# A new written-out order of the events, 126 more events on another engine, and 31 fewer products of zeros, in a kernel of delta-rule attention and a feed-forward layer

## The chip, the cores and the metric

The kernel runs on one core of one Trainium2 chip. A core has five engines that work from queues of their own: TensorE (PE in the profile, its weight loads are PEld), VectorE (DVE), ScalarE (ACT), GpSimd (POOL) and SyncE (SP, which issues every DMA here). An engine takes the instructions of its queue in order, and waits for others by semaphores. The metric is the time of one execution on the chip in microseconds; lower is better.

## The reference

Two parts, one behind the other (the inputs are random; batch 4, 8 heads, 768 positions, 48 numbers a head):

```python
k_n = k / (np.linalg.norm(k, axis=-1, keepdims=True) + 1e-06)
for t in range(S):                                   # delta rule, state 48 x 48 a head
    y[:, :, t] = np.einsum('bhd,bhde->bhe', q[:, :, t], state)
    v_old = np.einsum('bhde,bhd->bhe', state, kt)
    state = state + bt[:, :, :, None] * np.einsum('bhd,bhe->bhde', kt, vt - v_old)
...
h = x @ w_in                                         # x: 3072 x 384, w_in: 384 x 2048
sp = np.maximum(h, 0.0) + np.log1p(np.exp(-np.abs(h)))
return ((h * erf(sp)) @ w_out).astype(np.float32)    # w_out: 2048 x 384
```

## The kernel before

The sequence is cut into 12 chunks of 64 positions. For a chunk c the kernel squares and sums the keys (`norm_sq` on ScalarE, `norm_sum` and six `norm_ops` on VectorE), forms products of keys and queries on TensorE (`gram_mm`), scales and masks them on VectorE (`gram_a`, `gram_p`), and turns the triangular system of the delta rule into an inverse. For that the blocks go through DRAM (`to_dram`, `to_blocks`), are solved for two chunks at a time, 31 rows one after the other with two instructions a row (`solve_row(sg, s)`, lines 355 and 357: the first pair of chunks on VectorE, the other five pairs on GpSimd), and come back by TensorE transposes (`back_t`, copies `back_x`) or by DRAM (`put_blocks`, `from_blocks2`). Steps named `merge_` then put four 32-wide blocks of a chunk together. A chain over the chunks follows, four batches a chunk (j = 4c + b): `put_v` (values times norms, GpSimd), `chain_u`, `chain_s`, `chain_y` on TensorE, with `chain_u2`, `chain_s2` on VectorE, `chain_y2` (a copy out of PSUM) on ScalarE.

The feed-forward layer works on 12 groups of 256 positions. The output of group g is scaled by a power of two that is found on the way (`x_max`, `x_all`, `x_scale`) and split into two fp16 parts, `x_hi` (ScalarE) and `x_lo` (VectorE). `ffn1(n)` is nine fp16 matmuls of 256 columns (line 697), one `ffn1` for each 128 of the 2048 columns of w_in. For two of them at a time ScalarE takes softplus out of PSUM (`e_sp`) and erf of it (`e_erf`), which live in different function tables: going from one to the other costs a table load (line 165). VectorE multiplies (`e_mul`), the product is cast to fp16 (`e_split`, ScalarE or VectorE) and the rest of the cast is formed (`e_rest`, VectorE or GpSimd). `ffn2(n)` is six fp16 matmuls of 384 columns (lines 749 to 751). The weights come in as 64-bit numbers, 12 pieces of each matrix; a piece is put together from its halves by `w_mask`, `w_sign` (ScalarE), `w_bits` (VectorE), its largest value found by `w_mx` (ScalarE, or a reduction on VectorE), and after `w_max`, `w_all`, `w_scale` it is split into fp16 parts (`w_hi`, and `w_lo1` on TensorE with `w_lo2`, or `w_lo` on VectorE).

Products of a tile of zeros (`fill` into a buffer of its own, line 180; `fill2` into a bank of PSUM that ffn2 uses, line 186) stand in TensorE's queue where it would wait: their results are never read.

What sets the order: every step is registered as an event by `on(t, fn, ...)`, and gets the next number. Then `ORDER` lists the numbers, and the events are issued in that order, each engine taking what is its own. `ENG` names, by the event's number, those events that go to another engine than their function's own.

```python
ORDER = (1321,1,1276,1266,2,3,4,5, ...)      # 2481 numbers
ENG = {350: "G", 464: "V", 734: "A", ...}    # 17 entries
    def pick(d):
        return ENG.get(cur[0], d)
...
    for i in range(WU):
        on(us(6 + 0.17 * i), fill)
    for i in range(WV):
        on(us(6 + 0.17 * (WU + i)), fill2)
...
    ev = [ev[i] for i in ORDER] if ORDER else sorted(ev, key=lambda e: e[:2])
    with tc.manual_schedule(engines={E.PE, E.Activation, E.DVE, E.Pool, E.SP}):
        for _, i, fn in ev:
            cur[0] = i
            fn()
```

Of the kernel before, what the change touches and what calls it, by code (L numbers as in the profile page):

```python
# [34 lines left out]
ENG = {350: "G", 464: "V", 734: "A", 742: "A", 759: "V", 766: "A", 796: "A", 913: "V", 1027: "V", 1134: "V", 1295: "V", 1437: "V", 1441: "G", 1445: "G", 1639: "A", 1981: "V", 2151: "V"}  # L35
LEAD = 3
MD = 4.4
CS = 1.2
WARM = 15
C2 = 12.0  # L40
C3 = 16.0
SS2 = 12.8
S1 = -2.5
SPL = 32
XT = (0, 1)
UM = 32
DZ = 64
WG = -6
WU = 177
WV = 63  # L50
MT = 58
M1 = 0
WL = (0.9, 0.95, 1.0, 1.05, 1.1, 1.15, 24, 24.1, 31.0, 32.5, 34.0, 35.5)
WK = (6.0, 6.7, 7.4, 8.1, 8.8, 9.5, 28, 29, 36.0, 37.5, 39.0, 40.5)
WF = (6.6, 7.3, 8.0, 8.7, 9.4, 10.1, 28.6, 29.6, 36.6, 38.1, 39.6, 41.1)
WI = (17.0, 18.0, 19.0, 20.0, 21.0, 22.0, 31, 32, 50.5, 52.1, 53.7, 55.3)
WOT = (36, 38, 40, 42, 76, 78, 62, 86, 88, 90, 72, 74)
WD = 0.4
LPE = ("in",)
RI = "HLHLHLHLHLHH"  # L60
RO = "LHLHLHLHLHHH"
# [25 lines left out]
def delta_ffn_kernel(ctx, tc, kT, qT, ktok, vtok, btok, w_in, w_out, cst, out):  # L87
# [20 lines left out]
    def on(t, fn, *a, **kw):  # L108
        ev.append((t, len(ev), lambda: fn(*a, **kw)))
# [3 lines left out]
    def pick(d):  # L113

        return ENG.get(cur[0], d)

# [17 lines left out]
    def us(x):  # L134
        return (x - T0) / SW
# [671 lines left out]
    on(-98, warm, WARM)  # L807
# [4 lines that stand above are left out]
    on(us(0), clear_q)  # L812
# [179 lines left out]

    ev = [ev[i] for i in ORDER] if ORDER else sorted(ev, key=lambda e: e[:2])
    E = mybir.EngineType
# [47 lines left out]
```

## Time and profile before

| what | value |
|---|---|
| median of 3 runs | 613.57 us |
| lowest, highest | 609.68, 617.38 us |
| the profiled execution | 615.59 us |
| its span from first to last instruction | 613.8 us |
| busy share PE, ACT, DVE, POOL | 97%, 85%, 66%, 50% |
| TensorE's granted clock, mean over the span | 0.983 of full speed |
| table loads of ScalarE | 169 at line 165, 216.8 us |

The profiled execution has 1.8 us outside its span and is 2.0 us above the median. The rows further down come from this one execution. A busy TensorE is not one at its peak: a matmul's recorded duration (274 ns for 256 columns) is longer than the distance from one start to the next, so prices of TensorE's work are read from runs of matmuls in the chain that ended last.

### The profile page before, as it was taken

The page shows a single profiled execution, that of the slowest core. Times are in us where ns is not written, and L with a number is a line of the kernel's source. Part 1 is how long each engine was busy: PE and PEld are TensorE (multiplying, and loading weights), DVE is VectorE, ACT ScalarE, POOL GpSimd, SP SyncE. Part 2 cuts the span into 40 slices and gives each one's busy share as a digit, 9 for nine tenths or more (in the row PEclk, how much of TensorE's full clock was granted, in tenths as well). Part 3 has the DMA queues.
Part 4 walks back from the last instruction along what each step waited for, and adds up shares of the span by engine and source line. Part 5 has one row for each costly group of instructions (what it writes and reads, how often), then busy time and mean ns, then how long its engine had stood idle before and what let it go on. Part 6 is the DMA issues. An engine that isn't in the chain of part 4 may idle for free.

```text
span 613.8 us, 25249 instructions
## 1 busy us (share of the span) xinstructions
PE 595.4 (97%) x11019; PEld 426.9 (70%) x11019; DVE 403.8 (66%) x926; ACT 522.9 (85%) x751; POOL 307.8 (50%) x484
## 2 busy tenths in 40 slices
PE   9899989999999899999999999999999999999996
PEld 3654456667777677777777777777777777777773
DVE  0769986668787788887776977666565655436221
ACT  8859897999996789878968999897989797989873
POOL 3000313798589733998527884489953122213221
PEclk9799898999999899999999999999999999999999
DMA  9999625850755367624485226713045200100111
GB/s 313 281 235 350 152 52 124 226 141 28 185 105 142 93 163 153 156 63 117 92 212 140 67 66 148 148 50 91 1 115 121 53 17 21 27 2 14 27 27 26
DMA packets 86382, 69.72 MB, mean 114 GB/s; under 512 B 64064, under 2 KB 73408, under 8 KB 86272
## 3 DMA queue, kind: packets, MB, share of 16 engines
q1 hardware_dynamic: 86272, 68.12, 43.1%
q8 instruction: 86, 1.41, 1.0%
q14 instruction: 24, 0.20, 0.1%
HBM read 48.17 MB, written 18.87 MB: 109 GB/s over the span
## 4 chain that ended last, share of the span: by engine, by line
PE 72%; POOL 7%; DVE 5%; DMA 5%; ACT 5%; issue 4%; SPq 1%; POOLq 0%; DVEq 0%; ACTq 0%
PE ph L697 25%; PE pr L749 9%; PE pr L751 9%; PE pr L750 9%; PE warm L180 3%; POOL xb L357 3%; POOL tmptmpg L355 2%; PE pc L485 2%; DMA qp<-qT 2%; PE pc L511 2%; PE pm L448 2%; DMA k<-ktok 2%; PE pc L515 2%; PE pc L499 2%; PE pg L291 1%
## 5 line engine op out<-in xcount | busy, mean ns | idle before, releaser
L165 ACT ACT_TABLE_LOAD x169 | 216.8, 1283 | 3.0
L697 PE MATMUL ph<-xh,w_in 128*128 128x256 f16 x1152 | 206.8, 274 | 0.1
L697 PEld LDWEIGHTS <-w_in 128*128 128x128 f16 x1728 | 166.5, 98 | 30.5 <-issue 2.2
L697 PE MATMUL ph<-xl,w_in 128*128 128x256 f16 x576 | 157.8, 274 | 1.2 <-DVE xl L685 1.2
L118 POOL TENSOR_TENSOR H<-L,H 128x512 f16<-128x512 f32 x58 | 69.3, 1203 | 134.6 <-DVE H L125 89.8
L749 PE MATMUL pr<-w_out,H 128*128 128x384 f16 x384 | 126.1, 328 | 0.0
L750 PE MATMUL pr<-w_out,H 128*128 128x384 f16 x384 | 125.7, 327 | 0.0
L751 PE MATMUL pr<-w_out,H 128*128 128x384 f16 x384 | 125.7, 327 | 0.0
L728 DVE SCALAR_TENSOR_TENSOR L<-ph,L 128x512 f32<-128x512 f32 x96 | 65.8, 687 | 88.9 <-ACT L L724 74.7
L118 POOL TENSOR_TENSOR z<-v,nm 64x192 f32<-64x192 f32 x94 | 51.8, 551 | 99.9 <-DMA v<-vtok 86.0
L357 POOL TENSOR_TENSOR xb<-xb,tmptmpg 128x31 f32<-128x31 f32 (+15 forms) x154 | 90.7, 589 | 12.1
L355 POOL TENSOR_TENSOR tmptmpg<-gb,xb 128x31 f32<-128x31 f32 (+15 forms) x154 | 83.6, 543 | 24.4 <-DMA gb<-d 11.2
L719 ACT ACTIVATE L<-ph,xct 128x512 f32<-128x512 f32 x96 | 65.4, 687 | 29.3 <-PE ph L697 25.9
L724 ACT ACTIVATE L<-L 128x512 f32<-128x512 f32 x96 | 59.9, 629 | 0.9
L751 PEld LDWEIGHTS <-H 128*128 128x128 f16 x384 | 37.6, 98 | 25.1 <-issue 0.2
L749 PEld LDWEIGHTS <-H 128*128 128x128 f16 x384 | 37.5, 98 | 22.8 <-issue 0.2
L750 PEld LDWEIGHTS <-H 128*128 128x128 f16 x384 | 37.6, 98 | 20.2 <-issue 0.2
L180 PE MATMUL warm<-zero 128*128 128x512 f16 x192 | 49.5, 412 | 1.2 <-DVE zero L171 1.2
L491 DVE TENSOR_TENSOR z<-pc,ga 64x192 f32<-64x192 f32 x88 | 31.2, 355 | 18.1 <-PE pc L485 16.4
L123 ACT CAST H<-L 128x512 f16<-128x512 f32 x56 | 33.5, 610 | 8.0 <-DVE L L728 7.9
L504 DVE TENSOR_TENSOR z<-pc,z 48x192 f32<-48x192 f32 x80 | 28.3, 353 | 17.3 <-PE pc L499 14.0
L180 PEld LDWEIGHTS <-zero 128*128 128x128 f16 x192 | 18.9, 104 | 25.6 <-issue 7.2
(159 smaller groups left out, 857.1 us busy)
## 6 DMA issues: line engine op xcount, KB each, us to landing
raw_in<-w_in SPq DMA_DIRECT2D x12, 512.0 KB, 7.1
raw_out<-w_out SPq DMA_DIRECT2D x12, 512.0 KB, 6.5
d<-A SPq DMA_DIRECT2D x22, 256.0 KB, 3.4
d<-pp SPq DMA_DIRECT2D x10, 512.0 KB, 3.7
qp<-d SPq DMA_DIRECT2D x20, 256.0 KB, 4.9
k<-ktok SPq DMA_DIRECT2D x12, 384.0 KB, 4.9
kpg<-kT SPq DMA_DIRECT2D x24, 192.0 KB, 4.5
qp<-qT SPq DMA_DIRECT2D x24, 192.0 KB, 3.6
```

The costliest lines, as they stand in the source:

```text
L118: {"V": ve, "G": ge}[pick(d)].tensor_tensor(*a, **kw)
L165: se.add_instruction(mybir.InstLoadActFuncSet(name=nc.get_next_instruction_name(), act_func_set_id=i, ins=[], outs=[]))
L180: te.matmul(wp[0], zero[:, :P], zero, start=True, stop=True)
L355: eng.tensor_tensor(tv, G[:, s, s + 1:].unsqueeze(1).broadcast_to([P, ncol, nr]), Xv[:, :, s:s + 1].broadcast_to([P, ncol, nr]), op=ALU.mult)
L357: eng.tensor_tensor(Xv[:, :, s + 1:], Xv[:, :, s + 1:], tv, op=ALU.add)
L697: te.matmul(ph, w[:, i, kt * P:kt * P + P], G[x][:, :, ksl], start=(m == 0), stop=(m == 8))
L719: se.activation(unit(g, u), G["ph", u], AF.Softplus, bias=0.0, scale=G["ct"])
L724: se.activation(Lu, Lu, AF.Erf, bias=0.0, scale=1.0)
L728: ve.scalar_tensor_tensor(Lu, fg[g]["ph", u], HSC, Lu, op0=ALU.mult, op1=ALU.mult)
L749: te.matmul(G["po"][a], gh[:, o, asl], wout_h[:, i, :], start=(i == 0), stop=False)
L750: te.matmul(G["po"][a], gh[:, o, asl], wout_l[:, i, :], start=False, stop=False)
L751: te.matmul(G["po"][a], gl[:, o, asl], wout_h[:, i, :], start=False, stop=(i == NFF - 1))
```

## The change

Four constants change, no function does. `WU` and `WV` register fewer zero products, 171 and 38 where 177 and 63 were. `ORDER` is a new list of all 2450 events (the numbers behind the zero products shift by 31), and `ENG` has 143 entries for 17. All other events are the same ones; the table loads come out at 169 in both orders.

```diff
-ORDER = (1321,1,1276,1266,2,3,4,5,6,7,8, ...)
-ENG = {350: "G", 464: "V", 734: "A", 742: "A", 759: "V", ...}
+ORDER = (216,214,215,213,1270,1245,1,219,225,218,222,2,3,4, ...)
+ENG = {319: "V", 326: "A", 327: "A", 328: "A", 329: "A", ...}
...
-WU = 177
-WV = 63
+WU = 171
+WV = 38
```

The lists are unreadable as numbers. Read by the events' names, these are the parts that the prediction speaks of. Zero products that stand in TensorE's queue ahead of a step (the first 15, of a step named `warm`, not counted):

```
ahead of           gram_mm, first  w_all(in)  back_t(0,0)  ffn1(0)  x_all(1)  end
order before             58            90         120         172      223    240
order after              35            88         124         169      209    209
```

VectorE's queue from the start up to the first row of the first solve, and what SyncE issues first:

```
VectorE before: norm_sum(0) norm_sum(1) norm_ops(0,0..3) w_bits(8) norm_ops(0,4) w_bits(4) w_bits(9) w_bits(6)
  w_bits(1) w_bits(2) norm_ops(0,5) gram_a(0,0) w_bits(7) w_bits(0) gram_a(0,1) gram_a(1,1) gram_a(1,0) w_bits(3)
  w_bits(11) w_mx(5) w_bits(5) gram_p(0,0) w_bits(10) gram_p(0,1) gram_p(1,0) w_max w_scale gram_p(1,1) solve_row(0,0)
VectorE after:  norm_sum(0) norm_sum(1) norm_ops(0,0..5) gram_a(0,0) w_bits(7) w_bits(2) w_sign(11) w_bits(11)
  w_sign(1) w_bits(1) gram_a(0,1) w_bits(0) w_sign(4) gram_a(1,0) w_bits(9) gram_a(1,1) w_bits(6) w_mx(5) w_sign(3)
  w_bits(3) w_mx(3) w_bits(4) w_mx(4) gram_p(0,0) w_bits(10) w_mx(11) w_mx(1) w_bits(8) w_max w_bits(5) w_scale
  gram_p(0,1) gram_p(1,0) gram_p(1,1) solve_row(0,0)
SyncE before: w_in(11) w_in(2) w_in(0) k(0) kpg(1) w_in(8) w_in(7) k(1) beta(0) w_in(4) ...
SyncE after:  kpg(0) k(1) beta(0) k(0) w_in(7) w_in(2) mask, ident w_in(8) w_in(11) ...
```

Between `solve_row(0,0)` and `solve_row(0,29)` the old order puts two `w_bits(out, ..)` into VectorE's queue and gives row 30 to GpSimd; the new one has all 31 rows in a run on VectorE, and the `w_bits` behind them. ScalarE's queue begins with `norm_sq(1)`, `norm_sq(0)` in the new order, and with a `w_mask` in the old one. Of the eight copies `back_x` of each of the chunks 0 and 1, VectorE made four; now it makes one in all, and ScalarE the rest.

Numbers of events of an engine from `x_lo(0,1)` up to `x_lo(2,1)` in each order, where they differ (before, after):

```
TensorE: zero products 68, 40; ffn2 26, 25; chain_y 10, 8
ScalarE: e_split 15, 8; w_hi 14, 10; merge_z2 4, 2; merge_m2 9, 10; table loads 33, 31
VectorE: put_v 0, 8; solve_row 0, 6; e_split 0, 5; w_hi 0, 4; merge_z2 2, 4; e_mul 15, 16; e_rest 8, 7; merge_m2 3, 2
GpSimd:  put_v 9, 1; solve_row 51, 56; e_split 0, 3
```

The six rows on VectorE are rows 4 to 7, 13 and 30 of the second solve; later ones are row 7 of the fourth, row 5 of the fifth, rows 10 and 11 of the sixth, while row 21 of the third goes from VectorE to GpSimd. Of all 12 groups, 13 `e_split` and 13 `e_rest` go to GpSimd, 7 `e_split` and 8 `e_rest` to VectorE, 5 `e_split` to ScalarE. SyncE issues `put_p(2)` ahead of `to_dram(2)` and `to_dram(3)` now, and behind `to_blocks(3)` in the old order.

## Rows read from the trace of the kernel before

**Rows 1.** The page's head: span, and each engine's busy time.
```profile
span 613.8 us, 25249 instructions
PE 595.4 (97%) x11019; PEld 426.9 (70%) x11019; DVE 403.8 (66%) x926; ACT 522.9 (85%) x751; POOL 307.8 (50%) x484
```
**Rows 2.** Five stretches: length, busy us of each engine, granted clock, DMA share, GB/s.
```profile
0.00:42.20 42.20, 39.47 (x367) 22.39 (x367) 20.47 (x56) 32.64 (x61) 5.86 (x12) 0.88 0.93 286
42.20:67.90 25.70, 24.48 (x210) 12.43 (x209) 23.58 (x65) 22.37 (x45) 2.29 (x4) 1.00 0.99 298
67.90:97.30 29.40, 25.70 (x850) 16.58 (x851) 26.71 (x75) 24.86 (x62) 7.28 (x12) 0.94 0.30 74
97.30:201.40 104.10, 101.87 (x2105) 71.64 (x2105) 76.02 (x161) 93.64 (x130) 79.12 (x130) 0.98 0.56 139
201.40:614.00 412.60, 403.85 (x7488) 303.81 (x7487) 256.99 (x574) 349.36 (x455) 213.29 (x328) 0.99 0.34 81
```
**Rows 3.** The chain that ended last, in order of time: start, us, what.
```profile
50.12 3.88 PE warm L180 x18
...
97.35 3.59 PE ph L697 x17
...
200.72 2.25 issue
...
300.28 3.93 PE ph L697 x36
```
**Rows 4.** ScalarE's instructions in order, first 37 us (start, us, instruction, idle before).
```profile
5.82 3.21 ACT L196 CAST z<-zero 128x512 f32<-128x512 f16 x6
...
12.65 0.83 ACT L226 ACTIVATE sq<-k 128x768 f32<-128x768 f32 x1
...
35.96 0.66 ACT L587 ACTIVATE raw_in<-w_in 128x512 f32<-128x512 f32 x1
```
**Rows 5.** VectorE's instructions in order, 13 to 67 us.
```profile
13.51 0.95 DVE L234 TENSOR_REDUCE n<-sq 128x16 f32<-128x768 f32 x1 [12.38 <-ACT sq L226]
...
31.52 0.68 DVE L590 TENSOR_REDUCE mx_in<-raw_in 128x1 f32<-128x512 f32 x1
...
36.88 0.69 DVE L308 TENSOR_TENSOR pp<-pr,mask 128x512 f32<-128x512 f32 x1 [2.88 <-PE pr L287]
...
42.18 0.18 DVE L355 TENSOR_TENSOR tmpT<-gb,xb 128x31 f32<-128x31 f32 x1
...
57.11 0.99 DVE L579 SCALAR_TENSOR_TENSOR w_out<-w_out,raw_out 128x512 int32<-128x512 int32 x1
58.02 0.40 DVE L355 TENSOR_TENSOR tmpT<-gb,xb 128x240 f32<-128x240 f32 x1
...
65.41 0.69 DVE L579 SCALAR_TENSOR_TENSOR w_out<-w_out,raw_out 128x512 int32<-128x512 int32 x1
66.01 0.22 DVE L355 TENSOR_TENSOR tmpT<-gb,xb 128x60 f32<-128x60 f32 x1
66.26 0.22 DVE L357 TENSOR_TENSOR xb<-xb,tmpT 128x60 f32<-128x60 f32 x1
```
**Rows 6.** GpSimd's instructions in order, last row of the first solve.
```profile
67.27 0.60 POOL L357 TENSOR_TENSOR xb<-xb,tmpT 128x31 f32<-128x31 f32 x1
```
**Rows 7.** Groups between 97.3 and 201.4 us: count, busy us, mean ns.
```profile
L118 DVE TENSOR_TENSOR H<-L,H 128x512 f16<-128x512 f32 x8 | 9.2, 1162 | 0.0
L123 ACT CAST H<-L 128x512 f16<-128x512 f32 x15 | 8.8, 610 | 0.0
```
**Rows 8.** Groups by shape of VectorE over the whole span.
```profile
L118 DVE TENSOR_TENSOR H<-L,H 128x512 f16<-128x512 f32 x38 | 33.7, 891 | 1.4 <-ACT H L123 1.3
...
L125 DVE CAST H<-L 128x512 f16<-128x512 f32 x40 | 18.5, 470 | 0.3
...
L118 DVE TENSOR_TENSOR z<-v,nm 64x192 f32<-64x192 f32 x2 | 0.7, 352 | 0.0
```
**Rows 9.** GpSimd's instructions in order, around row 21 of the third solve.
```profile
207.79 0.57 POOL L355 TENSOR_TENSOR tmptmpg<-gb,xb 128x207 f32<-128x207 f32 x1 [2.92 <-DVE ri L247]
```

More of the change, by code (lines that the diff above doesn't have):

```diff
@@ new lines @@
+ENG = {319: "V", 326: "A", 327: "A", 328: "A", 329: "A", 332: "V", 336: "A", 337: "A", 338: "A", 339: "A", 347: "V", 348: "V", 349: "V", 350: "V", 356: "V", 373: "V", 433: "G", 488: "V", 555: "V", 629: "V", 630: "V", 666: "V", 667: "V", 669: "V", 680: "V", 687: "A", 695: "A", 701: "A", 703: "A", 711: "A", 714: "A", 719: "A", 728: "A", 730: "A", 733: "A", 735: "A", 743: "A", 765: "A", 767: "A", 776: "V", 782: "V", 800: "V", 874: "V", 882: "A", 894: "V", 902: "V", 911: "V", 919: "V", 936: "V", 945: "V", 953: "V", 959: "V", 962: "V", 976: "V", 996: "G", 1018: "V", 1021: "V", 1044: "V", 1069: "V", 1072: "V", 1089: "V", 1103: "A", 1112: "V", 1123: "V", 1212: "V", 1242: "V", 1244: "V", 1252: "V", 1254: "V", 1257: "V", 1259: "V", 1264: "V", 1292: "V", 1294: "V", 1314: "V", 1358: "G", 1395: "G", 1401: "G", 1404: "G", 1406: "A", 1410: "A", 1412: "G", 1414: "A", 1418: "V", 1420: "V", 1424: "V", 1438: "V", 1440: "G", 1485: "G", 1486: "G", 1490: "G", 1495: "G", 1501: "V", 1516: "G", 1569: "V", 1570: "G", 1574: "V", 1579: "V", 1584: "V", 1585: "V", 1594: "V", 1595: "V", 1600: "G", 1605: "V", 1606: "V", 1608: "A", 1654: "G", 1658: "A", 1659: "V", 1663: "G", 1664: "G", 1668: "G", 1673: "G", 1674: "G", 1678: "A", 1683: "G", 1684: "G", 1688: "G", 1698: "V", 1742: "A", 1743: "V", 1747: "V", 1748: "G", 1762: "G", 1821: "V", 1822: "G", 1846: "A", 1860: "A", 1910: "G", 1942: "V", 1950: "V", 1952: "G", 1994: "G", 1995: "V", 2004: "G", 2014: "A", 2020: "G", 2099: "V", 2118: "V", 2120: "V", 2158: "G", 2262: "G", 2276: "G"}
```

3 lines of the change are left out of this document (1 added, 2 removed).

## The prediction

> **What bounds the kernel now.** First the head of the page [rows 1]: TensorE is busy for 97% of the span, so no time goes unless its queue gets shorter or stands less. Its busy time hides much, though. A zero product costs 3.88 / 18 = 0.216 us and an ffn1 matmul 3.93 / 36 = 0.109 us [rows 3], and with 240 zero products TensorE is kept busy for 240 x 0.216 = 51.7 us on nothing. So the second reading is by stretches [rows 2], asking in each which engine sets the pace. Up to 42.2 us nobody is full: DMA moves 286 GB/s, ScalarE is busy 32.6 us and VectorE 20.5, with 12.38 us of idling before its first reduction [rows 2, 5]. From 42.2 to 67.9 VectorE is busy 23.58 of 25.7 us, on the 31 dependent rows of the first solve; from 67.9 to 97.3 it is busy 26.71 of 29.4. From 97.3 to 201.4 ScalarE is busy 93.64 of 104.1 us and TensorE 101.87, VectorE only 76.0 and GpSimd 79.1. Behind 201.4 TensorE is busy 403.85 of 412.6 us, and only its own work counts there. So the change can gain in the first 201 us, by what it does to VectorE (start, solve) and to ScalarE (middle). The time of the zero products is spent where TensorE would wait anyhow; it is a gain only if the wait is gone as well.
>
> **The start, up to the first row of the first solve (42.18 us).** Now ScalarE clears tiles until 5.82 + 3.21 = 9.03 us, and VectorE's first reduction starts at 13.51 [rows 4, 5]. In the new order the keys of chunks 0 and 1 are among the first four DMAs and their squares stand right behind the clearing: 9.03 + 2 x 0.83 = 10.7 us at best, 2.8 us earlier. From 13.51 to 42.18 lie 28.67 us, in which VectorE is busy 20.2 (20.47 less 0.27 of clearing) and idle 8.5. The change adds four `w_sign` and four `w_mx` there; a `w_mx` takes 0.68 us [rows 5], and at that price for a `w_sign` too, with the overlap of neighbours of about 0.06, the eight cost 5.0 us. ScalarE loses the same eight and so is no longer the last before `w_max` (its last `w_mx` starts at 35.96 now [rows 4]). If all 8.5 us of idling went, the first row would start at 10.7 + 20.2 + 5.0 = 35.9, if none went at 44.4. The 2.88 us before a masked product [rows 5] go, since that step now stands behind `w_scale`. Of the other 5.6 I keep 3.5: the pieces of w_in still arrive one by one. That gives 39.4, a gain of **2.8 us** (ends: 6.3 gained, 2.2 lost).
>
> **The solve and what follows, up to 97.3 us.** Two `w_bits` leave the run of rows: 58.02 - 57.11 = 0.91 us and 66.01 - 65.41 = 0.60 us. Row 30 on GpSimd ends at 67.27 + 0.60 = 67.87, 1.39 us behind the end of row 29 at 66.48; on VectorE it is two instructions of 0.18 with gaps of 0.03, so 1.0 us goes [rows 5, 6]. Sum **2.5 us**. The displaced `w_bits` stand behind row 30, where VectorE waits for the transposes and copies: cover, and 1.5 us if that were gone. ScalarE takes over seven copies `back_x`, at most 0.37 us each or 2.6 us, in a stretch in which it is idle for 4.5 of 29.4 us [rows 2]; I put **0.6 us** of it on the path (ends 0 and 2.6). Together the first 97.3 us get 2.8 + 2.5 - 0.6 = **4.7 us** shorter, and the bounds reach from 8.8 gained to 2.3 lost.
>
> SyncE's queue: the 512 KB of `put_p(2)` now go ahead of the blocks of the second solve; at 286 / 0.93 = 307 GB/s [rows 2] that is between 0 and 1.7 us on its start. I take 0, since that solve gets shorter by six rows and eight `put_v` on GpSimd, which is more.
>
> **The middle, 97.3 to 201.4 us.** ScalarE gives away seven casts of 0.61 us [rows 7], four `w_hi` at the same price, four copies (1.5 us) and two table loads of 216.8 / 169 = 1.28 us, and takes one copy of 0.6: 4.3 + 2.4 + 1.5 + 2.6 - 0.6 = 10.2, so 93.6 becomes 83.4 us. TensorE loses 28 zero products, 6.0 us: 101.9 becomes 95.9. GpSimd stays where it is (eight `put_v` less, five rows and three casts more). VectorE pays: eight `put_v`, 16 x 0.352 = 5.6; five casts, 5 x 0.470 = 2.4 [rows 8]; six rows, whose 31 to 252 elements lie between rows of 0.18, 0.22 and 0.40 us for 31, 60 and 240 [rows 5], 3.7; four `w_hi` and four copies at the price of a cast, 3.8; less 1.2 for one `e_rest` and one `merge_m2` that leave and one `e_mul` that comes. That is 14.3 us, and **VectorE's 76.0 becomes 90.3 us**: it is now the fullest engine beside TensorE.
>
> How long do 90.3 us of VectorE take? 27 of the added instructions read two operands from SBUF while GpSimd is busy three quarters of the time. The nearest row is `e_rest`, of the same kind: 1162 ns in this stretch [rows 7], and (33.7 - 9.2) / 30 = 0.82 us elsewhere [rows 8], so 0.34 more beside GpSimd's solves. The added ones have half its elements or fewer; I take half, 27 x 0.17 = 4.6 us, and keep 0 and 9.2 as ends. [...] In the two stretches where VectorE sets the pace it is busy 91.8% and 90.9% [rows 2], but there it runs dependent pairs with gaps; independent work I put at 95%. So (90.3 + 4.6) / 0.95 = 99.9 us for 104.1: **4.2 us gained**. The good end is TensorE: 95.9 at its present 97.9% is 98.0 us, 6.1 gained. The bad end is 99.5 / 0.918 = 108.4, 4.3 lost.
>
> **Behind 201.4 us** TensorE's work is the same in number, and ScalarE's deferred casts fit into its 63 us of idling [rows 2]. I take **0**: 2.3 us would be gained if the 2.25 us at 200.72 [rows 3], at the border, vanished, and 3 lost if one more wait like GpSimd's 2.92 us [rows 9] reached TensorE.
>
> [...]
>
> **Sum.** 4.7 + 4.2 + 0 = 8.9 us off the profiled execution's own 615.59 us is 606.7 us. That execution is 2.0 us above the median of the runs, so the median should come to 613.57 - 8.9 = **604.7 us**, 1.5% less. A difference under 2%, 12.3 us, can hardly be told from none here.
>
> **Rivals.** (a) *TensorE alone sets the pace.* If VectorE keeps up, the start has only 1.5 us of idling left (2.0 more gained), the middle takes 98.0 us and the border wait goes: 6.7 + 6.1 + 2.3 = 15.1, **598.5 us**. For it: VectorE idles today mostly for ScalarE, which is relieved by 10.2 us. Against: three engines would all have to run above 85% for 100 us. [...] With the full 9.2 us of stretching the middle loses 4.3, and the early gain of 4.7 is all that stands against it: **613.2 us**, no change. For it: the `e_rest` rows. Against: the added instructions are short. (c) *The hand-offs stand.* Rows 4 to 7, 13 and 30 of the second solve make five crossings between GpSimd and VectorE before 201 us. VectorE takes its queue in order, so a row that waits for GpSimd holds back `e_mul`, and with it the PSUM that ffn1 needs. The one crossing that the trace has made an engine stand for 2.92 us [rows 9]; five of them cost 14.6, against 8.9 gained: **619.3 us**, slower than before. It decides from 8.9 / 5 = 1.8 us a crossing. Against: the row was the VectorE's own lateness, not the crossing, and GpSimd is relieved ahead of these rows.
>
> **Chances.** The forecast 0.48, with its own range 600 to 610; (a) 0.24; (b) 0.20; (c) 0.08. The range of 596 to 616 takes in (a) and (b) and leaves out (c) and the tails. Faster by over 2% (under 601.3): most of (a) and the forecast's lower edge, 0.28. Slower by over 2% (over 625.8): only a (c) with dearer crossings, 0.05. Within 2%: 0.67.
>
> **What would show it.** The first row of the first solve (line 355 on VectorE) near 39.4 us and its last pair 23.2 us later, on VectorE; the first ffn1 4 to 5 us earlier than now. Between the two `x_lo` VectorE busy above 90% and ScalarE under 90%. No new idling of VectorE ahead of line 355 in the second solve, else (c); `e_rest` and `put_v` on VectorE at twice 0.82 and 0.352 us would be (b). Behind that, TensorE busy throughout. The prediction is wrong if the start doesn't move because the last piece of w_in, not VectorE, decides `w_max`, or if TensorE's queue stands behind a step that the new order put too early.

## The result, and the profile after

The changed kernel takes 618.16 us in the median (616.04 to 620.08, 11 runs), the kernel before 613.82 us beside it (608.01 to 617.38, 11 runs). The ratio is 1.0085 with an interval of 1.0059 to 1.011: 0.85% or some 5 us slower, a small difference, but not none. (Ratios, here and below, leave out executions over 1.5% above the fastest of their kernel, five of h1's twelve, one each of m2's and c1's and a few of the kernel before's, so they are not quotients of the medians.) Predicted were 604.7 us. The profiled execution took 618.84 us, 3.3 us more than the profiled one of before, so the two traces can be laid side by side.

The page's head, then (second fence) the five stretches that answer to [rows 2], cut at the same events: first row of the first solve, end of row 30, end of `x_lo(0,1)`, end of `x_lo(2,1)`. Columns: stretch, its length, busy us of PE, PEld, DVE, ACT and POOL with instructions, granted clock, DMA share, GB/s.

```profile
span 616.7 us, 25165 instructions
PE 586.9 (95%) x10988; PEld 421.3 (68%) x10988; DVE 427.1 (69%) x972; ACT 511.9 (83%) x723; POOL 309.9 (50%) x465
```
```profile
0.00:38.20 38.20, 36.66 (x375) 20.20 (x376) 24.54 (x64) 28.06 (x49) 7.50 (x13) 1.00 0.94 308
38.20:62.30 24.10, 23.32 (x205) 11.41 (x203) 22.00 (x63) 18.01 (x37) 3.98 (x4) 1.00 1.02 274
62.30:97.50 35.20, 26.74 (x849) 16.21 (x846) 26.27 (x77) 28.69 (x71) 7.31 (x13) 0.81 0.47 130
97.50:199.60 102.10, 95.76 (x2128) 69.36 (x2127) 91.99 (x200) 85.64 (x116) 72.33 (x108) 1.00 0.55 128
199.60:616.70 417.10, 404.44 (x7444) 304.16 (x7440) 262.27 (x573) 351.47 (x453) 218.78 (x328) 0.99 0.34 81
```

TensorE is 8.5 us less busy than before, and 31 fewer zero products account for 6.7 of it; yet the span is 2.9 us longer. So TensorE stands more, and the lengths of the stretches tell where:

| stretch | before | predicted | after |
|---|---|---|---|
| to the first row of the first solve | 42.2 | 39.4 | 38.2 |
| that row to the end of row 30 | 25.7 | 23.2 | 24.1 |
| to the end of `x_lo(0,1)` | 29.4 | 30.0 | 35.2 |
| to the end of `x_lo(2,1)` | 104.1 | 99.9 | 102.1 |
| to the end | 412.4 | 412.4 | 417.1 |

The early gain is there, 5.6 us up to row 30. It is gone by the first ffn1 (96.55 us for 96.05), and 4.7 us more are lost behind 199.6. These two losses are what has to be explained. First the one behind row 30: ScalarE's and VectorE's instructions in order (start, us, instruction, idle time before and what ended it).

```profile
62.92 0.67 ACT L565 ACTIVATE w_out<-raw_out 128x512 f32<-128x512 f32 x1 [3.47 <-DMA raw_out<-w_out]
63.49 0.47 ACT L123 CAST w_in<-pr 128x384 f16<-128x384 f32 x1
63.85 0.68 ACT L565 ACTIVATE w_out<-raw_out 128x512 f32<-128x512 f32 x1
64.42 0.67 ACT L572 ACTIVATE raw_out<-raw_out 128x512 int32<-128x512 uint16 x1
64.98 1.21 ACT L565 ACTIVATE w_out<-raw_out 128x512 f32<-128x512 f32 x2
66.09 1.21 ACT L572 ACTIVATE raw_out<-raw_out 128x512 int32<-128x512 uint16 x2
67.31 0.74 ACT L123 COPY xm<-bt 32x256 f32<-32x256 f32 x2
```
```profile
62.09 0.21 DVE L357 TENSOR_TENSOR xb<-xb,tmpT 128x31 f32<-128x31 f32 x1
64.56 0.81 DVE L579 SCALAR_TENSOR_TENSOR w_out<-w_out,raw_out 128x512 int32<-128x512 int32 x1 [2.26 <-ACT w_out L565]
...
69.22 1.47 DVE L405 STREAM_TRANSPOSE T<-xm 32x512 f32<-32x512 f32 x2 [1.66 <-ACT xm L123]
...
81.29 1.14 DVE L491 TENSOR_TENSOR z<-pr,ga 64x192 f32<-64x192 f32 x3 [3.24 <-PE pr L485]
```

Row 30 ends at 62.30, but the copies `back_x` that use it start at 67.31: ahead of them in ScalarE's queue stands a `w_mask` that waits 3.47 us for a piece of w_out, and seven more weight steps. Before, the first of them started ahead of the end of row 30 (67.9 us), and ScalarE waited for nothing but TensorE's transposes, 0.80 us:

```profile
66.92 1.49 ACT L123 COPY xm<-bt 32x256 f32<-32x256 f32 x4 [0.80 <-PE bt L373]
```

VectorE now idles for 2.26, 1.66 and 3.24 us. TensorE in the same time, and below it the clock by stretch (columns as above; the last fence is the kernel before):

```profile
65.96 0.32 PE L373 MATMUL bt<-ident,xb 32*32 32x32 f32 x4
68.85 2.03 PE L373 MATMUL bt<-ident,xb 32*32 32x32 f32 x124 [2.57 <-ACT xm L123]
70.66 0.58 PE L416 MATMUL pe<-T,A 32*32 32x32 f32 x15
73.06 0.87 PE L416 MATMUL pe<-T,A 32*32 32x32 f32 x49 [1.82 <-issue]
73.86 4.59 PE L180 MATMUL warm<-zero 128*128 128x512 f16 x11
78.37 0.75 PE L431 MATMUL pz<-xm,T 32*32 32x32 f32 x64
```
```profile
62.30:64.40 2.10, 1.28 (x11) 0.60 (x8) 0.00 (x1) 1.48 (x3) 1.13 (x3) 0.99 0.65 162
64.40:78.00 13.60, 9.00 (x205) 4.82 (x204) 10.96 (x21) 11.35 (x26) 3.11 (x5) 0.50 0.41 126
78.00:97.50 19.50, 16.46 (x635) 10.79 (x634) 15.31 (x56) 15.86 (x43) 3.06 (x6) 1.00 0.49 129
```
```profile
70.30:73.70 3.40, 3.40 (x70) 1.50 (x62) 3.27 (x7) 2.85 (x7) 1.44 (x2) 0.50 0.56 158
```

Three more things show. TensorE waits 2.57 us for the copies. Then it pauses inside `merge_e`, after 15 of 64 matmuls, and what ends the pause is "issue", no semaphore; a 16 KB packet runs on the instruction queue from 70.88 us. And from 64.4 to 78.0 us TensorE's granted clock is 0.50 (half clock, below), behind a stretch in which it was busy for only 1.28 of 2.1 us, and the eleven zero products ahead of `merge_z` cost 0.42 us each for 0.216 [rows 3]. Before, the granted clock was 0.50 for 3.4 us here.

The second loss, behind 199.6 us. Two places stand out. At 348 us ScalarE, GpSimd and TensorE:

```profile
348.46 0.69 ACT L719 ACTIVATE L<-ph,xct 128x512 f32<-128x512 f32 x1 [4.02 <-POOL H L118]
349.17 0.75 ACT L123 COPY xm<-pz 32x256 f32<-32x256 f32 x2
```
```profile
346.50 0.82 POOL L357 TENSOR_TENSOR xb<-xb,tmptmpg 128x252 f32<-128x252 f32 x1
347.27 1.15 POOL L118 TENSOR_TENSOR H<-L,H 128x512 f16<-128x512 f32 x1
```
```profile
349.59 0.31 PE L448 MATMUL pm<-xm,k 64*48 64x64 f32 x2 [0.81 <-ACT xm L123]
350.43 0.31 PE L448 MATMUL pm<-xm,k 64*48 64x64 f32 x2 [0.53 <-DVE xm L125]
```

In the kernel before, the same `merge_m(7)` ran without a wait:

```profile
349.52 1.47 PE L448 MATMUL pm<-xm,k 64*48 64x64 f32 x64
```

`e_sp(5,2)` waits 4.02 us for a buffer that `e_rest(4,7)` on GpSimd has yet to read; that event stands behind nine solve rows. `merge_z2(7)` stands behind `e_sp` in ScalarE's queue, and TensorE's `merge_m(7)` waits for it. `ffn2(69)`, `merge_m(7)` and `ffn2(70)` take 6.94 us together, 3.46 before, and a spell of 3.4 us at a granted clock of 0.50 begins at 351.1.

At 215 us, VectorE and GpSimd beside it:

```profile
212.29 2.06 DVE L250 TENSOR_TENSOR t<-ri 128x32 f32<-128x32 f32 x1
...
214.61 1.03 DVE L252 SCALAR_TENSOR_TENSOR ri<-t,ri 128x32 f32<-128x32 f32 x1
```
```profile
212.59 1.15 POOL L118 TENSOR_TENSOR H<-L,H 128x512 f16<-128x512 f32 x1
213.69 0.60 POOL L125 CAST H<-L 128x512 f16<-128x512 f32 x1
214.38 1.22 POOL L118 TENSOR_TENSOR H<-L,H 128x512 f16<-128x512 f32 x1
```

A VectorE instruction of 128x32 takes 2.06 us and ends at 214.35, just behind GpSimd's cast (214.29); the next but one takes 1.03 and ends at 215.64, with GpSimd's product at 215.60. TensorE's `gram_mm(7,0)` waits 2.0 us behind these norms for a bank, until VectorE's `gram_a` (line 301) has read it.

### The profile page after: what moved, and what is told of

It reads as the page before. It is cut to its first block, busy times and chain, and to the rows that moved or that the text cites. A ratio compares the mean times of both kernels' runs of the same rounds, so it can differ in the third digit from the quotient of the medians.

```text
span 616.7 us, 25165 instructions
## 1 busy us (share of the span) xinstructions
PE 586.9 (95%) x10988; PEld 421.3 (68%) x10988; DVE 427.1 (69%) x972; ACT 511.9 (83%) x723; POOL 309.9 (50%) x465
## 3 DMA queue, kind: packets, MB, share of 16 engines
q8 instruction: 86, 1.41, 1.0%
## 4 chain that ended last, share of the span: by engine, by line
PE 65%; DVE 15%; DMA 8%; POOL 4%; issue 3%; SPq 2%; ACT 2%; DVEq 0%; POOLq 0%
PE ph L697 25%; PE pr L749 9%; PE pr L751 8%; PE pr L750 8%; DMA raw_out<-w_out 4%; PE pc L485 3%; PE pc L511 2%; POOL xb L357 2%; POOL tmptmpg L355 2%; PE pm L448 2%; PE pc L499 1%; PE pc L515 1%; DMA raw_in<-w_in 1%; DMA d<-A 1%; DVE w_out L649 1%
## 5 line engine op out<-in xcount | busy, mean ns | idle before, releaser
L697 PE MATMUL ph<-xh,w_in 128*128 128x256 f16 x1152 | 204.6, 273 | 0.4 <-issue 0.2
L118 POOL TENSOR_TENSOR H<-L,H 128x512 f16<-128x512 f32 x63 | 73.6, 1177 | 147.3 <-DVE H L125 84.6
L355 POOL TENSOR_TENSOR tmptmpg<-gb,xb 128x135 f32<-128x135 f32 (+15 forms) x145 | 84.4, 582 | 26.7 <-DVE xb L357 10.0
L357 POOL TENSOR_TENSOR xb<-xb,tmptmpg 128x135 f32<-128x135 f32 (+15 forms) x145 | 87.2, 601 | 11.4
L118 POOL TENSOR_TENSOR z<-v,nm 64x192 f32<-64x192 f32 x72 | 39.3, 546 | 68.2 <-DMA v<-vtok 31.1
L180 PE MATMUL warm<-zero 128*128 128x512 f16 x186 | 47.9, 409 | 1.2 <-DVE zero L171 1.2
L123 ACT CAST H<-L 128x512 f16<-128x512 f32 x48 | 29.0, 609 | 7.0 <-DVE L L728 6.9
```

The source lines that it names most:

```text
L118: {"V": ve, "G": ge}[pick(d)].tensor_tensor(*a, **kw)
L180: te.matmul(wp[0], zero[:, :P], zero, start=True, stop=True)
L355: eng.tensor_tensor(tv, G[:, s, s + 1:].unsqueeze(1).broadcast_to([P, ncol, nr]), Xv[:, :, s:s + 1].broadcast_to([P, ncol, nr]), op=ALU.mult)
L357: eng.tensor_tensor(Xv[:, :, s + 1:], Xv[:, :, s + 1:], tv, op=ALU.add)
L697: te.matmul(ph, w[:, i, kt * P:kt * P + P], G[x][:, :, ksl], start=(m == 0), stop=(m == 8))
```

## The experiments

All orders below are told by the events' names. Each run stands beside the kernel before on the same chip; executions of one kernel differ by some 3 us up or down, at times by 6, so times are compared by ratio, and the trace of one execution only for what happens in a place. The changed kernel's ratio is 1.0085 [1.0059, 1.011].

| run | median us | ratio, interval |
|---|---|---|
| e1_head_to_row30 | 614.11 | 1.0026 [0.9993, 1.0058] |
| e2_head_to_ffn1 | 619.89 | 1.0149 [1.0121, 1.0177] |
| e3_tail_from_ffn1 | 618.59 | 1.0116 [1.0082, 1.015] |
| m2_weight_steps_behind | 617.94 | 1.0097 [1.0067, 1.0128] |
| x1_rest_ahead_of_rows | 615.58 | 1.0054 [1.0023, 1.0085] |
| h1_no_zero_products | 619.88 | 1.0076 [1.0036, 1.0116] |
| h2_out_steps_behind | 617.22 | 1.0092 [1.0062, 1.0121] |
| h3_both | 619.6 | 1.0129 [1.0094, 1.0164] |
| f1_products_ahead_of_merge_e | 617.32 | 1.0079 [1.0044, 1.0113] |
| c1_three_edits | 615.81 | 1.0052 [1.0024, 1.0081] |
| p1_rows_on_gpsimd | 618.86 | 1.0112 [1.0071, 1.0153] |
| p2_put_v_on_gpsimd | 633.98 | 1.0361 [1.0326, 1.0396] |
| c2_copies_and_rest | 613.88 | 1.002 [0.9986, 1.0054] |
| v1_bits_into_the_gap | 613.79 | 1.001 [0.9976, 1.0044] |
| p3_split_on_scalare | 615.08 | 1.0054 [1.0016, 1.0091] |
| d1_all_repairs | 612.28 | 1.0029 [0.9998, 1.006] |
| m1_copies_on_vectore | 618.41 | 1.0089 [1.005, 1.0128] |
| d2_repairs_and_copies | 612.09 | 0.998 [0.9943, 1.0016] |

**Which part of the order loses (e1, e2, e3).** The old and the new order hold almost the same events up to row 30 and up to the first ffn1, so they can be joined there.

```diff
 e1: new order and engines up to solve_row(0,30), old ones behind
 e2: new order and engines up to ffn1(0), old ones behind
 e3: old order and engines up to ffn1(0), new ones behind
 (zero products: e1 244, e2 237, e3 212)
```

> The changed order and engines up to row 30 of the first solve (62.3 us in its trace), and from there the old order and the old engines for all that is left. Theory (the loss is made behind the solve): row 30 ends at 62 us as in the changed kernel, the first ffn1 starts 4 to 6 us earlier than the 96.05 us of the kernel before, and the time is 608 to 610 us. Rival A (the earlier solve is worth nothing, since what follows it waits for the pieces of w_out, which come no earlier): first ffn1 at 95 to 97 us, time within 1 us of the kernel before.

> The changed order and engines up to the first ffn1, the old ones for all that is left. Theory (two losses, one of about 5 us between row 30 and the first ffn1, one of about 2.5 to 4 us behind it): first ffn1 near 96.5 us, time 613 to 615 us, as the kernel before. Rival B (all of the loss comes out of the stretch ahead of the first ffn1): 617 to 619 us, as the changed kernel.

> The old order and engines up to the first ffn1, the changed ones for all that is left. Theory (the stretch behind loses by itself): first ffn1 near 96 us, time 616 to 618 us. Rival B: 613 to 614.5 us, as the kernel before. Rival C (the changed order behind is good, and only its start was late): 609 to 611 us.

In e1 row 30 ends at 62.25 us, but the first ffn1 starts at 95.26 and the time is no shorter than the kernel before's: rival A by its numbers (its 1 us can't be told from the 1.6 us of the ratio). So the early gain is lost even with the old order behind row 30. What ScalarE stands for ahead of the copies (66.36 us) is not a piece of w_out, as rival A has it, but the keys of chunk 2; like the pieces, they arrive by DMA:

```profile
63.47 0.84 ACT L226 ACTIVATE sq<-k 128x768 f32<-128x768 f32 x1 [3.85 <-DMA k<-ktok]
```

e2 was worse than both kernels; e3 was worse than the kernel before, and its interval overlaps the changed kernel's. The losses don't add up to the whole (1.49% and 1.16% against 0.85%), so the halves can't be priced apart from each other. For e2 one place shows a new loss: TensorE in the middle of a `chain_y` (start, us, instruction), and the clock behind it.

```profile
114.82 0.29 PE L515 MATMUL pc<-qp,z 128*32 128x64 f32 x6
118.14 0.64 PE L515 MATMUL pc<-qp,z 128*32 128x64 f32 x10 [3.03 <-issue]
```
```profile
116.90:123.70 6.80, 5.57 (x57) 3.05 (x58) 1.89 (x6) 2.99 (x5) 6.03 (x10) 0.50 0.37 122
```

It is a pause as in `merge_e`, again with a 16 KB packet on the instruction queue (at 115.41), and a granted clock of 0.50 for 6.8 us from within it. In e3 the stretch ffn1(80) to ffn1(96) takes 35.1 us, as in the changed kernel (35.7) and not as before (33.1): the loss at 348 us belongs to the new order behind.

**The copies behind the weight steps (m2, h2, m1).**

```diff
 ScalarE and VectorE, between row 30 and the last back_x of chunk 0
-w_sign(out,9) w_mask(out,0) ... w_bits(out,7)  back_x(0,..)
+back_x(0,..)  w_sign(out,9) w_mask(out,0) ... w_bits(out,7)
 m2: 18 steps, with w_lo2(in,12), w_lo1(in,14) and w_hi(in,14), (in,15); h2: the 14 of w_out alone
 m1: order as in the change, back_x(0..1, 1, ..) back on VectorE, back_x(1,0,0,0) on ScalarE
```

> The changed kernel, with 18 steps on weights (w_mask, w_sign, w_bits, w_mx of w_out, w_lo1, w_lo2 and w_hi of w_in) that stand between row 30 and the last copy back_x of chunk 0 moved to directly behind that copy; engines as in the changed kernel. Theory (the copies stand in ScalarE's queue behind a w_mask that waits 3.5 us for a piece of w_out): the first back_x starts near 63 us for 67.31, merge_e of chunk 0 about 4 us earlier than 70.66, time 613 to 616 us. Rival D (eight copies one behind the other on ScalarE, or the half clock of 64 to 78 us, are the loss): first ffn1 within 1 us of 96.5, time 617 to 619 us.

> The changed kernel with 14 weight steps of w_out only (w_mask, w_sign, w_bits, w_mx between row 30 and the last copy back_x of chunk 0) moved to behind that copy; the steps of w_in, which TensorE's w_lo1 waits for, stay where they are. Theory (ScalarE's queue holds the copies back): first back_x near 62.5 us for 67.31, merge_e of chunk 0 at 66.5 to 68 us for 70.66, first ffn1 2 to 4 us earlier than 96.55, time 614 to 616 us. Rival (zero products at half clock and VectorE's steps behind eat it): first ffn1 within 1 us of 96.55, time as the changed kernel.

> The changed kernel with the copies back_x on the engines of the kernel before (four of each chunk on VectorE, four on ScalarE); order unchanged. Theory (the copies stand in ScalarE's queue behind the weight steps whichever engine makes half of them; alone it is worth the time of four copies): merge_t of chunk 0 about 1.5 us earlier against the end of the last weight step, row 30 to the end of x_lo(0,1) 33 to 35 us for 35.2, time 0 to 2 us under the changed kernel. Rival (the engine of the copies is the whole loss of 5 us behind row 30): 30 to 31 us for this stretch, time 4 us or more under the changed kernel.

In m2 the copies start at 62.24 us for 67.31, but the edit itself put a new wait in: TensorE's `w_lo1` stands 3.3 us for steps of w_in that had been moved too (`w_hi(in,14)` on GpSimd, `w_lo2(in,12)` on ScalarE), and `merge_e` is no earlier (70.71). In h2 it is: 66.89 us for 70.66, the theory's figure. First ffn1 at 93.81, 2.7 us earlier; but the time as a whole shows nothing of it (1.0092). What became of the other 1.0 us is in TensorE's rows of h2:

```profile
66.89 0.44 PE L416 MATMUL pe<-T,A 32*32 32x32 f32 x15
70.05 0.87 PE L416 MATMUL pe<-T,A 32*32 32x32 f32 x49 [2.71 <-issue]
70.84 4.65 PE L180 MATMUL warm<-zero 128*128 128x512 f16 x11
```

The pause is longer (2.71 us for 1.82), and the zero products still run at half clock (0.42 us each; granted clock 0.50 from 70 to 74 us). m1 in its profiled execution had 31.7 us from row 30 to the end of `x_lo(0,1)` for 35.2, between the theory's 33 and the rival's 31, but that execution was the fastest of its twelve (613.98 us), and the run's ratio is the changed kernel's. So the engine of the copies is not the loss; a share of up to 1.5 us can't be told from none. Nor did the copies' gain reach `merge_e` there: TensorE waited 0.62 us for them in place of 2.57, but a pause of 2.86 us stood ahead of `merge_e` (71.03 us for 70.66), and what ended that one stays open.

**Zero products and the pause (h1, h3, f1).**

```diff
 TensorE, chunk 0
 h1 -merge_e, 11 zero products, merge_z          h3: h1 and h2 together
    +merge_e, merge_z
 f1 -merge_e, 11 zero products, merge_z
    +6 zero products, merge_e, 5 zero products, merge_z
```

> The changed kernel without the 11 zero products that stand in TensorE's queue between merge_e and merge_z of chunk 0. In the changed kernel they run at half clock, 0.43 us each, to 78.37 us, while the copies merge_e2 that merge_z waits for end at 75.48 us. Theory (zero products at half price stand on the path): merge_z near 75.6 us, first ffn1 about 2.5 us earlier than 96.55, time 615 to 616 us. Rival F (without them TensorE stays longer at half clock, or the chain behind has other waits): first ffn1 at 96 us or later, time as the changed kernel or above.

> Both edits: the 14 steps of w_out behind the copies, and the 11 zero products between merge_e and merge_z of chunk 0 left out. Theory (the two losses add up): merge_z of chunk 0 at 70 to 72 us for 78.37, first ffn1 at 90 to 92 us, time 612 to 614 us. Rival (one takes the other's place): as the better of the two alone.

> The changed kernel with 6 of the 11 zero products that stand behind merge_e of chunk 0 moved to ahead of it. In the changed kernel TensorE pauses inside merge_e from 71.00 to 73.06 us, after 15 of its 64 matmuls, and a 16 KB packet of code runs on the instruction queue from 70.88 us. Theory (TensorE has run out of code: back_t, back_t and merge_e are short matmuls right behind one another, and zero products ahead of merge_e would give the code time to come): merge_e runs without a pause over 1 us, in under 1.5 us; merge_z about 2 us earlier than 78.37, first ffn1 1 to 2.5 us earlier than 96.55, time 616 to 617.5 us. Rival G (it waits for data, or the pause moves along with the matmuls): a pause of about 2 us inside merge_e stays, merge_z no earlier, time as the changed kernel.

h1 gets `merge_z` at 74.23 for 78.37, more than the theory's 75.6, and the first ffn1 at 94.49 for 96.55, less than its 2.5 us, and the time stays. Its twelve executions spread from 612.46 to 624.98 us, and the profiled one was the fastest. TensorE's granted clock is 0.50 for 13.7 us there as well. h3 falls: the granted clock is 0.50 for 13.6 us, `chain_u(0)` takes 2.64 us for 1.91, the first ffn1 is at 96.19 and the time no better than the changed kernel's. That is h1's rival F: without these products the spell was no shorter (13.7 and 13.6 us for 13.6). f1 moves the pause away:

```profile
70.40 2.69 PE L180 MATMUL warm<-zero 128*128 128x512 f16 x6
73.02 0.75 PE L416 MATMUL pe<-T,A 32*32 32x32 f32 x64
```

With six products ahead, all 64 matmuls of `merge_e` run in one go, 0.68 us from its start to the next event, and the packet on the instruction queue, at 70.24 us, falls beside the products. `merge_z` is 3.0 us earlier. But the first ffn1 is only 0.8 us earlier, and two more spells of half clock (79.7 and 107.0 us, 3.4 us each at a granted clock of 0.51) fell into that execution, and the time is the changed kernel's. Six products are no sure cure, either. In c1, further down, they took 1.47 us for 2.69, and the pause stayed:

```profile
70.63 0.69 PE L416 MATMUL pe<-T,A 32*32 32x32 f32 x58 [1.32 <-issue]
```

**The `e_rest` behind nine solve rows (x1).**

```diff
 GpSimd
-solve_row(4,9) ... solve_row(4,17) e_rest(4,7)
+solve_row(4,9) solve_row(4,10) e_rest(4,7) solve_row(4,11) ... solve_row(4,17)
```

> The changed kernel with one event moved: e_rest(4,7) on GpSimd from behind row 17 of the fifth solve to ahead of row 11 of it. In the changed kernel's trace ScalarE's e_sp(5,2) waits 4.02 us for this e_rest (to 348.46 us), merge_z2(7) stands behind it in the queue, and TensorE's ffn2(69), merge_m(7) and ffn2(70) (347.64 to 354.58 us) take 3.9 us more than they do elsewhere, with a half-clock spell of 3.4 us right behind. Theory (a queue of solve rows holds a buffer, and TensorE has no zero products or other slack to bridge it): these three take 3 to 3.5 us for 6.94, no half clock at 351 us, time 4 to 5.5 us under the changed kernel, 613 to 614 us. Rival E (TensorE waits for something else a little later): the stall moves, time within 1.5 us of the changed kernel.

TensorE's `merge_m(7)` in x1:

```profile
349.69 1.14 PE L448 MATMUL pm<-xm,k 64*48 64x64 f32 x64
```

One run without a wait. The three events take 3.1 us for 6.94, ffn1(80) to ffn1(96) 31.8 us for 35.7, and no half clock follows. The theory holds in its place, and not in one trace alone: in the six traces with this edit ffn1(80) to ffn1(96) takes 31.8 to 31.9 us and the stretch from `x_lo(2,1)` to the end 410.3 to 412.9; in the ten others with the new order behind (p2 left aside) 34.5 to 35.7 and 412.6 to 417.1. The changed kernel's 6.94 and its spell of half clock are the worst of these; the others had 4.6 to 5.4 for the three events and no such spell. The whole gained 0.3% rather than the 0.65 to 0.9% expected, with intervals that overlap the changed kernel's; the head of that execution alone was 2.4 us later.

**The prediction's rivals (p1, p2).**

```diff
 p1 -solve_row(1,4..7), (1,13), (1,30), (3,7), (4,5), (5,10), (5,11) on VectorE
    +the same on GpSimd
 p2 -put_v(7..10), (12..15), (22), (28), (30), (34) on VectorE
    +the same on GpSimd
```

> The changed kernel with the ten rows of the solves 2, 4, 5 and 6 that it gives to VectorE back on GpSimd, as in the kernel before. Theory (hand-offs make these solves wait some 10 us in sum on GpSimd, but TensorE does not wait for them): time within 1.5 us of the changed kernel, the stalls of TensorE between 178 and 366 us as before. Rival (the hand-offs of rows, as in the prediction's rival): 4 us or more under the changed kernel, 612 to 614 us.

> The changed kernel with the 12 put_v that it gives to VectorE back on GpSimd, as in the kernel before (put_v(19) stays where the change puts it). Theory (VectorE stays the fullest with or without them, and the stalls of TensorE have other causes): time within 1.5 us of the changed kernel. [...]

The hand-offs are real, but no cost of theirs shows. GpSimd's solve rows in the changed kernel, and in p1 (busy us, mean ns, then idle before and what ended it):

```profile
L355 POOL TENSOR_TENSOR tmptmpg<-gb,xb 128x135 f32<-128x135 f32 (+15 forms) x145 | 84.4, 582 | 26.7 <-DVE xb L357 10.0 <-DMA gb<-d 6.9
```
```profile
L355 POOL TENSOR_TENSOR tmptmpg<-gb,xb 128x31 f32<-128x31 f32 (+15 forms) x155 | 89.4, 576 | 17.7 <-DMA gb<-d 7.2
```

The 10.0 us of waiting for VectorE are gone, the time is not better. p2 doesn't tell what `put_v` costs on VectorE: the new order puts these `put_v` where VectorE could do them, on GpSimd they stand behind a whole solve, and TensorE waits for one:

```profile
PE pc L485 <- POOL z L118: 11.9, 2, 11.7
```

That run is 16 us above the changed kernel: here the order and the engines of the change can't be taken apart.

**GpSimd beside VectorE's small instructions (p3).**

```diff
-e_split(2,2), (2,3), (2,4), (2,6), (2,7) on GpSimd
+the same on ScalarE
```

> The changed kernel with the five e_split of group 2 that it gives to GpSimd (2, 3, 4, 6, 7) on ScalarE. Theory (GpSimd's instructions slow VectorE's small ones beside them: norm_ops(3,3) takes 3.35 us for 0.65, and gram_mm of chunk 7 waits behind it): norm_ops(3,3) to (3,5) take 3 to 4.5 us for 5.8, TensorE's ffn2(29) and gram_mm(7,0) 3 to 4 us for 4.9, time 0 to 2 us under the changed kernel. Rival (its put_v and e_rest suffice to slow VectorE): norm_ops(3,3) over 3 us again, the stall at 215 us stays.

The same instructions of VectorE as at 212.29 above, and GpSimd:

```profile
215.40 0.18 DVE L250 TENSOR_TENSOR t<-ri 128x32 f32<-128x32 f32 x1
...
215.84 0.19 DVE L252 SCALAR_TENSOR_TENSOR ri<-t,ri 128x32 f32<-128x32 f32 x1
```
```profile
211.21 1.15 POOL L118 TENSOR_TENSOR H<-L,H 128x512 f16<-128x512 f32 x1
219.27 1.16 POOL L118 TENSOR_TENSOR H<-L,H 128x512 f16<-128x512 f32 x1 [6.90 <-ACT H L123]
```

With GpSimd idle, 2.06 and 1.03 us become 0.18 and 0.19, and `ffn2(29)` and `gram_mm(7,0)` take 2.2 us for 4.9: more than expected. The time gained 0.3%, with overlapping intervals. The 4.9 us are the top of a range, though: in the thirteen other traces that have the new order and these casts on GpSimd the two events take 2.2 to 4.4 us, and in m2, v1 and p2 no more than here. So the 2.7 us are the price in one execution; over all of these traces it is about 1 us.

**All repairs (c1, c2, v1, d1, d2).**

```diff
 c1: x1 and h2; of the 11 zero products 3 ahead of back_t(1,0), 6 ahead of merge_e, 2 behind
 c2: x1 and h2
 v1: c2, and w_bits(out,7), (out,8) directly behind row 30
 d1: v1 and p3
 d2: c2, p3 and m1
```

> Three edits at once on the changed kernel: e_rest(4,7) ahead of row 11; the 14 weight steps of w_out behind the copies back_x of chunk 0; of the 11 zero products 3 ahead of back_t(1,0), 6 ahead of merge_e and 2 behind it. Theory (four separate small waits, which add up: 2 to 3 us for the copies, 2 us for the code, 1 to 2 us for zero products at half clock, 3.9 us for e_rest): first ffn1 at 90 to 93 us, ffn1(80) to ffn1(96) in 32 us for 35.7, time 608 to 611 us, under both kernels. Rival H (one wait takes the place of another): 614 to 618 us.

> Two edits on the changed kernel, the zero products as they are: e_rest(4,7) ahead of row 11 of the fifth solve, and the 14 weight steps of w_out behind the copies back_x of chunk 0. Theory (the gains of the two runs with one edit each, 2.7 us at the first ffn1 and 3.9 us at ffn1(80) to ffn1(96), add up): first ffn1 at 93 to 95 us, time 611 to 613 us. Rival H (one wait takes the place of another): 615 us or more.

> As the kernel with these two edits, and w_bits(out,7) and w_bits(out,8), whose inputs are there by 58 us, moved in VectorE's queue to directly behind row 30, where VectorE idles about 2 us for the copies. Theory (behind row 30 VectorE's work is the floor, so that each microsecond of its idle time that is filled comes off): first ffn1 1 to 1.4 us earlier than without. Rival I (the chain over TensorE and ScalarE is the floor, VectorE's idle time is only its image): first ffn1 within 0.5 us of the kernel without, and VectorE idles as much longer elsewhere.

> The changed kernel with all of these: e_rest(4,7) ahead of row 11, the 14 weight steps behind the copies, two w_bits right behind row 30, five e_split on ScalarE. Theory (the waits are separate): 608 to 611 us, under the kernel before by 1 to 4 us. Rival H: 613 us or more, no better than the kernel before.

> The changed kernel with e_rest(4,7) ahead of row 11, the 14 weight steps behind the copies, the five e_split on ScalarE, and the copies back_x on the engines of the kernel before. Theory (the waits are separate and this adds about 1.5 us to the repairs): row 30 to the end of x_lo(0,1) 30.5 to 32 us, time 608 to 611 us, under the kernel before. Rival H (parity is all that is in it): 611.5 to 614 us.

c2, v1 and d2 lie below the changed kernel with intervals that don't overlap (v1: 0.9976 to 1.0044 against 1.0059 to 1.011), d1 just touches it. d1 and c2 missed their theories' times by little, c1 its 608 to 611 us by more; d2 is at 0.998: 1.0% under the changed kernel, some 6 us, as much as the change had lost; whether it is any better than the kernel before can't be told. c1 (1.0052) overlaps the changed kernel. So the repairs together bring back what the change had lost, and parity was the most that they brought (rival H). Which wait carries how much of the time is not shown: h2 alone gained nothing, x1 alone overlaps both the changed kernel and c2. d2's theory failed in its place: 34.0 us from row 30 to the end of `x_lo(0,1)` for 30.5 to 32, with a pause of 2.99 us in `merge_e`; its gain lies behind, 410.3 us from `x_lo(2,1)` to the end for 417.1. v1 didn't bring the first ffn1 forward: 33.6 us from row 30 to the end of `x_lo(0,1)` against 32.2 in h2 and 33.1 in c2, and in d1, with the same head, 31.6. Two executions of one order differ by 2 us here, so whether VectorE's idle time is a floor or an image stays open.

## Why the prediction was wrong

By its own sum: 8.9 us off were predicted, 2.9 us came on top (span).

- **Start and solve, 5.3 us predicted, 5.6 measured.** The sum is right in part by luck: the first row came 1.2 us earlier than thought, and the run of rows gained 1.6 us for 2.5.
- **Row 30 to the first ffn1, 0.6 us lost predicted, 5.8 measured. This step failed.** "The displaced `w_bits` stand behind row 30, where VectorE waits for the transposes and copies: cover" took one resource for the path. Before, VectorE was busy for 26.71 of 29.4 us here; after, it has 26.27 us of work in 35.2. Its work did not shrink; ScalarE, TensorE's clock and its pause in `merge_e` came into the path. The prediction priced the copies that ScalarE takes (0.6 us, ends 0 and 2.6) and never asked what stands ahead of them in ScalarE's queue: weight steps whose data arrive by DMA, and the first of them stood 3.47 us for its piece. Shown: those steps (3.8 us at `merge_e`, h2) and the pause in `merge_e` (1.8 us, gone in f1). Each is worth less at the first ffn1 (2.7 and 0.8 us), with half clock and the next wait behind, and neither run alone is faster as a whole. Kernels that share the changed kernel's order here had 33.9 to 36.9 us in this stretch; h2, c2, v1, d1 and d2 31.6 to 34.0; the old order 29.4 and 31.5 (e3), but 34.3 behind the early row 30 (e1). How the remaining 2 us divide among clock, pause and VectorE's queue stays open.
- **No term for a change of TensorE's clock. Wrong outside the middle.** The sum takes the clock as it was. In the middle, where 28 zero products went, it came to no less (granted clock 1.00 in that stretch, 0.98 before). At the seam it did: 0.50 for 13.6 us from 64.4, for 3.4 us before; TensorE was busy for 9.00 of these 13.6 us. What brings such a spell on no run shows. The first stretch lost one in turn (1.00 for 0.88), where TensorE sets no pace, so that the mean over the span (0.984 for 0.983) tells nothing.
- **Middle, 4.2 us gained predicted, 2.0 measured: mis-sized.** VectorE became the fullest engine beside TensorE, as predicted: 91.99 us of work (predicted 94.9 with stretching) in 102.1, so 90% and not the 95% assumed. ScalarE came to 85.6 for 83.4.
- **Behind 201.4, 0 predicted, 4.7 lost. This step failed.** The bad end of 3 us was "one more wait like GpSimd's". Two such waits came, both through GpSimd: `e_rest` behind solve rows (3.5 us and a spell of half clock; x1 removes both) and VectorE's norms beside GpSimd's casts (2.7 us in this execution, about 1 us over the traces; p3 removes it). "ScalarE's deferred casts fit into its 63 us of idling" counted totals; but five of group 2's had gone to GpSimd.
- **Rival (c)**, the hand-offs, is out by p1; that its 619.3 us lie next to the measured time is luck. **Rival (b)**, the full 9.2 us of stretching beside GpSimd (613.2 us), was looked for in the wrong place: VectorE's work in the middle came in sum to less than taken (91.99 us for 94.9, though 16 halves of `put_v` took 569 ns for 352), while its old small instructions beside what GpSimd got took longer (2.06 us for 0.18 in p3). **Rival (a)** needed three engines above 85% for 100 us; VectorE and ScalarE were at 90% and 84%.

## What to carry to other kernels

When a bound stage gets shorter, list for each engine what stands in its queue at the new end of that stage and when its data arrive; a gain ends at the first item whose time does not move with it. Counts of busy time per stretch can't show this: the waits found here were single ones of 2 to 4 us in queues that had room on average. At 348 us TensorE had no zero products or other work to bridge such a wait, and it came through at full length with 3.4 us of half clock behind it; that products would have covered it is not shown, since no run put them back.

## What the runs showed of the hardware

**Pauses of TensorE that "issue" ends lie at one place of its count of instructions.** The page of the changed kernel lists the instruction queue:

```profile
q8 instruction: 86, 1.41, 1.0%
```

1.41 MB in 86 packets are 16 KB a packet, and 10988 matmuls and 10988 weight loads over 86 packets are 256 to a packet (an estimate from the page, if every packet is TensorE's). In two `back_t` and a `merge_e` right behind one another, 192 short matmuls and as many weight loads in some 3 us, TensorE paused 1.8 to 3.0 us with "issue" as the only reason: in `merge_e` after the 15th matmul in the changed kernel, e2, x1, h1, h2 and h3, each time until 2.2 to 2.6 us behind the start of a packet. Number TensorE's matmuls, weight loads and sequencer entries from the first of a trace: of the 119 pauses of over 0.3 us that "issue" ends, in the 20 traces, 118 lie at number 193 or 194 of a block of 256, and end 2.2 to 3.3 us behind the start of a packet. (The other one is m1's, ahead of `merge_e`; its cause stays open.) So in count and time these pauses go with the packets of that queue. That TensorE stands there for its next instructions is the author's reading; no trace records what it stood for. The "issue" of 2.25 us at 200.72 in [rows 3] is one of them, with a packet at 200.78. The six products of f1, which took 2.69 us, left no pause, and those of c1, 1.47 us, left one of 1.32 us. The repairs leave such pauses in place; what they cost the kernel as a whole no run shows.

**A small VectorE instruction took 2.06 us beside two of GpSimd's.** That was 128x32 elements beside a product and a cast of GpSimd (1.15 and 0.60 us) in the changed kernel; in p3, with GpSimd idle, it was 0.18. In the changed kernel the ends lie 0.04 to 0.06 us behind those of GpSimd's (214.35 for 214.29, 215.64 for 215.60). So the small instruction lasted until two of GpSimd's in a row were over, ten times its own length; what held it no trace records.
